# An attention and MLP kernel in which the first chunk's blocks travel before the second chunk's loads

## The chip, the cores and the metric

The kernel runs on one core of a Trainium2 chip. The metric is the time of one execution on the device in microseconds (us), the median of several runs. The data are float32 throughout.

## The reference

Two stages follow each other. The first is a recurrence (rwkv7) over 768 tokens, for 4 batches of 8 heads with 40 channels; the second is an MLP with a SiLU over all 3072 rows of 320 channels (8 heads x 40), with 2048 hidden channels.

```python
for t in range(S):
    y[:, :, t] = einsum('bhd,bhde->bhe', rt, state)
    Sa = einsum('bhde,bhe->bhd', state, at)
    state = state * wt[:, :, None, :] - einsum('bhd,bhe->bhde', Sa, bt) + einsum('bhd,bhe->bhde', vt, kt)
...
x = y.transpose(0, 2, 1, 3).reshape(B * S, H * D)
h = x @ w_in
out = (h * (1.0 / (1.0 + exp(-h)))) @ w_out
```

The two weight matrices come as 64-bit floats; the kernel gets them as pairs of 32-bit words.

## The kernel before

**Tiling.** The recurrence is cut into 12 chunks of 64 tokens. A chunk has two units (two batches each), which the code calls `units[n][m]`. Within a chunk the recurrence becomes a triangular system of 64 x 64 per batch and head; its inverse is built, and only the state goes from chunk to chunk.

**A chunk's steps and the engines they use.**
- *load* (L200, L215): a (256 KB), b and k (two halves of 128 KB each), w (two halves of 128 KB); *load_rv* (L442) brings v in two layouts (v2, vl), its transpose (vut) and r.
- *pre* (L247): `scale` makes running products of w by two scans (L254) and a reciprocal (L255) on VectorE, and multiplies a and b by them on GpSimd (L256, L257). `keys` does the same for k (L263) and sums squares on ScalarE (L266, L267). `scores` makes 64 x 64 products on TensorE (L230), masks them on VectorE into `sb` (L238), and, after the second unit, sends their 32 x 32 diagonal blocks to the DRAM tile `md` in four DMAs (L278).
- *inverse* (L295): `mi` is read back from `md` (L310), so that a block lies in one partition. For the first four chunks 15 row steps of one multiplication and one reduction each (L316, L322) on VectorE invert 16 x 16 halves; `back` turns the result, half on ScalarE (L330), half on VectorE (L331), and writes it to the DRAM tile `xd` (L332).
- *merge* (L337): four DMAs read `xd` into `XT` (L347), four VectorE transposes follow (L353), then products and copies that make 32 x 32 inverses of the 16 x 16 ones (L360 to L398, with VectorE at L368 and L393), and 64 x 64 ones of those (`first` L410 and L420, `second` L427 and L437).
- *chain* (L465): `keys` transposes (L476) and copies (L477), `right` (L238 into `sk`, L498, L508), `solve` (L520 to L546), `read` (L574, L582), `write` (L606, updates of the state Gbd L619, L623, outputs yx L628, which go to DRAM), `turn` (L558, L567).
- *moe* (L642): `first` multiplies by w_in (L669, L674), takes a sigmoid on ScalarE (L677) and multiplies on VectorE into `gts` (L678); `second` multiplies by w_out (L685).
- *weights* (L157): 40 pieces of the weights are converted from 64-bit words, each by two VectorE operations (L161, L162), three of ScalarE (L163 to L165) and three of VectorE (L170, L172, L173). Pieces pass through a few tiles named `room`; when one is done, the load of a later one is issued (L176).

**What sets the order.** The main program (L745 to L821) calls these steps in the order of the code; a scheduler arranges each engine's instructions from that, once, when the program is built. `tc.issue_after(x)` keeps what is in it behind x. `weave` mixes lists of steps. `in_order` (L185) chains TensorE's MoE products; the scans and reciprocals of chunk 0 are kept in program order (L251). Chunks 0 and 1 are inverted alone, all later ones in pairs. While chunk 0 is inverted, chunk 1's `prepare` runs, so its loads and scans stand early.

**Queues.** DMAs are issued by SyncE (SP) and ScalarE (ACT). Loads are SyncE's, except the four w of chunks 0 and 1, at the very start. The transfers md, mi, xd and XT of chunks 0 and 1 are ScalarE's, which executes them between its computations; those of later chunks are SyncE's. All loads of chunks 0 and 1, of the first five pieces of weights, of r and v and of chunk 2's b and k are issued at the start with no wait other than for a place. The two queues share eight completion semaphores, each used again only when the DMA before it on it has landed.

Of the kernel before, what the change touches and what calls it, by code (L numbers as in the profile page):

```python
# [41 lines left out]
def kernel(  # L42
# [95 lines left out]
    def load_weights(n, queue=nc.sync):  # L138

        if n == 0:  # L140
            rooms["gts"] = [sb.tile([128, 2, 4 * WS], I32, name="room2", tag="gts", bufs=2) for _ in range(2)]
        if n < NG and n % 5 < 4:
            rooms[n] = rooms["gts"][n % 5 // 2][:, n % 5 % 2]
        else:
            tag = "room" if n < NG else ("room", "mi", "tmp")[n % 3]
            rooms[n] = sb.tile([128, 4 * WS], I32, name="room", tag=tag)
        for lo, hi, src in pieces[n][1]:
            raw = rooms[n][lo:hi, 0 : 2 * WS]
            queue.dma_start(raw.rearrange("p (i x) -> p i x", x=256) if len(src.shape) == 3 else raw, src)
# [30 lines left out]
    def behind(x, ins):  # L180

        info = mybir.DependencyInfo(mybir.DependencyClass.NoSync, mybir.DependencyReason.DATA)
        tc.add_manual_dep(x.ins, ins.name, info, reason="in order")

    def in_order(x):  # L185

        if "last" in issued:
            behind(x, issued["last"])
        issued["last"] = x.ins
# [10 lines left out]
    def load(u, what="abk"):  # L200
        B2 = slice(2 * u.m, 2 * u.m + 2)
        if "a" in what:
            u.a = sb.tile([128, Q, C], F32, name="a", bufs=4)
            nc.sync.dma_start(
                u.a.rearrange("p (b q) t -> p b (q t)", b=2), aT[B2, u.n].rearrange("b p c -> p b c")
            )
        if "b" in what:
            u.kb = sb.tile([128, Q, 2, C], F32, name="kb", bufs=6)
        for n, x in ((1, bT), (0, kT)):
            for be in range(2 if "kb"[n] in what else 0):  # L210
                nc.sync.dma_start(
                    u.kb[:, P * be : P * be + P, n], x[2 * u.m + be, u.n].rearrange("p (q t) -> p q t", q=P)
                )

    def load_w(u, at, queue=nc.sync):  # L215
        u.w = at
        for be in range(2):
            queue.dma_start(
                at[:, P * be : P * be + P, 1 : C + 1], wT[2 * u.m + be, u.n].rearrange("p (q t) -> p q t", q=P)
            )  # L220

    def between(u, n, s):
# [14 lines left out]
        for j in range(2):  # L237
            nc.vector.tensor_tensor(  # L238
                out=s[:, j],
                in0=pm[j][:, 0 : P * C].rearrange("p (q t) -> p q t", q=P),  # L240
                in1=ms[:, n].unsqueeze(1).to_broadcast([128, P, C]),
                op=ALU.mult,
            )

    sbs, mark = {}, {}

    def pre(u, md):  # L247
        def scale():
            u.W = sb.tile([128, Q, C + 1], F32, name="W", bufs=6)
            R = u.w[:, :, 1 : C + 1]  # L250
            pin = tc.keep_in_program_order if u.n == 0 else lambda x: x  # L251
# [6 lines left out]
            if u.n > 0:  # L258
                keys()
# [9 lines left out]
        def scores():  # L269
# [3 lines left out]
            queue = nc.scalar if u.n < 2 else nc.sync  # L273
            for be in range(2 if u.m == NM - 1 else 0):
                for c in range(2):
                    at = 64 * (u.n % 2) + 16 * (2 * be + c)
                    r = C * be + 32 * c
                    x = queue.dma_start(  # L278
# [3 lines left out]
                    if u.n == 1:  # L282
                        behind(x, mark["mi"])
# [4 lines left out]
        return [scale, scores] + ([keys] if u.n == 0 else [])  # L288
# [6 lines left out]
    def inverse(md, N, queue, lo=0, hi=128):  # L295
# [13 lines left out]
        for h in range(lo, hi, 64):  # L309
            mark["mi"] = queue.dma_start(mi[h : h + 64], md[h : h + 64]).ins  # L310
        L = slice(lo, hi)

        def row(t):
            n = N - 1 - t
            part = tmp[L, :, 0:n, 0:n]
            nc.vector.tensor_tensor(  # L316
# [5 lines left out]
            last = nc.vector.tensor_reduce(out=X[L, :, t + 1 : N, t], in_=part, axis=AX.X, op=ALU.add)  # L322
            mark["row"] = last.ins
# [4 lines left out]
        def back():  # L328
            turned = XI.rearrange("p t s -> p s t")
            nc.scalar.copy(out=mi[L, 0:16], in_=turned[L, 0:16])  # L330
            nc.vector.tensor_copy(out=mi[L, 16:32], in_=turned[L, 16:32])  # L331
            queue.dma_start(xd[L], mi[L])  # L332
# [4 lines left out]
    def merge(n, xd, queue):  # L337
# [4 lines left out]
        def fetch():  # L342
            for be in range(2):
                at = 64 * (n % 2) + 32 * be
                for c in range(2):
                    r = C * be + 32 * c
                    queue.dma_start(  # L347
                        X[r : r + 32, :, 32 * c : 32 * c + 32],
                        xd[at + 16 * c : at + 16 * c + 16].rearrange("q s t -> s q t"),
                    )  # L350
            for r in range(0, 128, 32 if small(n) else 64):
                c = r % 64
                nc.vector.transpose(out=X[r : r + 32, :, 32 - c : 64 - c], in_=X[r : r + 32, :, c : c + 32])  # L353

        def sixteen(s, pp):

            pa = bank("pq")
# [10 lines left out]
            nc.vector.tensor_scalar(  # L368
                out=pp, in0=pa[:, 0 : N * 16].rearrange("p (h t) -> p h t", h=N), scalar1=lower, scalar2=None, op0=ALU.mult
            )  # L370
# [21 lines left out]
            for r in range(0, 128, 64):  # L392
                nc.vector.tensor_tensor(  # L393
                    out=X[r : r + 32, :, 32:48], in0=pe[r : r + 32, 1], in1=X[r : r + 32, :, 32:48], op=ALU.add
                )
# [4 lines left out]
        def first():  # L400
            s = sbs[n].rearrange("p m j q t -> p (m j q) t")
            both = sb.tile([128, N, 48], F32, name="qq", tag="tmp")
            box["qq"] = both[:, :, 0:32]
            if small(n):
                sixteen(s, both[:, :, 32:48])
# [12 lines left out]
            for be in range(2):  # L418
                R = slice(C * be + 32, C * be + 64)
                nc.scalar.copy(out=box["qq"][R], in_=pq[be][R, 0 : N * 32].rearrange("p (h t) -> p h t", h=N))  # L420

        def second():
            po = [bank("po") for _ in range(2)]
            for h in range(N):
                for be in range(2):
# [3 lines left out]
                        lhsT=box["qq"][r + 32 : r + 64, h, :],  # L429
# [9 lines left out]
        return [fetch, first, second]  # L439


    def load_rv(u):  # L442
        u.v2 = sb.tile([128, H, D], F32, name="v2", bufs=2)
        u.r = sb.tile([128, Q, C], F32, name="r", bufs=2)
# [5 lines left out]
        for be in range(2):  # L450
            nc.sync.dma_start(u.v2[C * be : C * be + C].rearrange("p h d -> p (h d)"), v[2 * u.m + be, T, :])
        for be in range(2):
            nc.sync.dma_start(
                u.vl[0:C, P * be : P * be + P, :, 0:D].rearrange("s p j d -> s (p j) d"),
                v[2 * u.m + be, T, :].rearrange("s (h d) -> s h d", d=D),
            )
        for be in range(2):
            nc.sync.dma_start(
                u.vut[:, P * be : P * be + P, 0], vT[2 * u.m + be, u.n].rearrange("p (q t) -> p q t", q=P)
            )  # L460
        nc.sync.dma_start(
            u.r.rearrange("p (b q) t -> p b (q t)", b=2), rT[B2, u.n].rearrange("b p c -> p b c")
        )

    def chain(u, xs):  # L465
# [4 lines left out]
        def keys():  # L470
            u.kt = sb.tile([128, Q, 128], F32, name="kt", bufs=2)
            for i in range(2):
# [4 lines left out]
                nc.scalar.copy(out=u.kt[:, 4 * i : 4 * i + 4].rearrange("p q e -> p (q e)"), in_=pt)  # L477

        def right():
# [26 lines left out]
            for be in range(2):  # L506
                R = slice(C * be, C * be + C)
                nc.scalar.copy(  # L508
                    out=rhs[R, :, :, 0:D],
                    in_=pr[be][R, 0 : H * D].rearrange("p (q j d) -> p q j d", q=P, j=2),  # L510
                )

# [207 lines left out]
    def invert(n, chunks=2):  # L720
# [11 lines left out]
        def do(k, i):  # L732
            if i == 0:
                box[k] = merge(k, box["xd"], queue)
            box[k][i]()

        late[n if chunks == 1 else n - 1] = [partial(do, n, 1), partial(do, n, 2)]
# [4 lines left out]
            + [partial(do, k, i) for k in each[:-1] for i in (1, 2)]  # L742
# [8 lines left out]
    for u, at in zip(units[0] + units[1], [w0] + early):  # L751
        load_w(u, at, nc.scalar)
    for n in range(2):
        for what in "ab", "k":
            for u in units[n]:
                load(u, what)
    for n in range(3):
        load_weights(n)
    for u in units[0]:
        load_rv(u)  # L760
    for n in range(3, 5):
        load_weights(n)
    for u in units[2]:
        load(u, "bk")
    convert = [partial(weights, n) for n in range(NW + 1)]

# [5 lines left out]
    run(prepare(1))  # L772
    chains = {0: [chain(u, xs) for u in units[0]]}
    run([x[i] for i in range(2) for x in chains[0]])
    run(convert[0:4] + rows[1:17])
    queue = []
    with tc.issue_after(mark["row"]):
        run(rows[17:])
        rows = invert(1, 1)
        run(late.pop(0))  # L780
        run(rows)
        for u in units[2]:
            load(u, "a")
        steps = [x for pair in zip(*[x[2:] for x in chains[0]]) for x in pair]
        steps[6:6] = late.pop(1)
        weave(steps, convert[4:21])
        for u in units[1]:
            load_rv(u)
# [6 lines left out]
        issued["last"] = mark["right"].ins  # L795
# [8 lines left out]
    for n in range(2, NN):  # L804
        for u in units[n]:
            load_rv(u)
# [170 lines left out]
```

## Time and profile before

| | |
|---|---|
| median of 5 runs | 953.76 us (952.9 to 960.2) |
| the profiled execution | 957.42 us, span 955.3 us |
| mean granted clock of TensorE | 0.918 |
| TensorE (PE) busy | 828.0 us, 87% |
| VectorE (DVE) busy | 565.8 us, 59% |
| ScalarE (ACT) busy | 291.2 us, 30% |
| GpSimd (POOL) busy | 97.4 us, 10% |
| data moved | 83.06 MB, 87 GB/s in the mean |

The profile counts an engine as busy while it computes; issuing a DMA is not counted. A page has the span in 40 slices of 23.9 us, where a digit is the busy share in tenths; windows give the same in microseconds for stretches that one chooses, with the number of instructions in brackets. The chain of waits goes back from the last instruction: each row is a start, a duration, and what the next row waited for. Groups and tiles give the durations of single instructions.

### The profile page before, as it was taken

What the parts mean: (1) busy time and instruction counts of PE and PEld (TensorE: products, weight loads), DVE (VectorE), ACT (ScalarE), POOL (GpSimd) and SP (SyncE); (2) the same over time, 40 slices, a digit from 0 to 9 for tenths busy, and PEclk for the clock granted to TensorE, in tenths of its full rate; (3) what the DMA queues carried; (4) which work ended last, traced back from release to release, by engine and by line L of the source; (5) the groups of instructions that cost most, each with busy time, mean ns of one, the idle gap of its engine ahead of it and who ended that gap; (6) DMA issues with size and microseconds to landing.
All of it is one profiled execution on the core that took longest, in us unless ns stands there. A gap on an engine that the chain in (4) does not pass through costs nothing.

```text
span 955.3 us, 26541 instructions
## 1 busy us (share of the span) xinstructions
PE 828.0 (87%) x11586; PEld 584.0 (61%) x11586; DVE 565.8 (59%) x1141; ACT 291.2 (30%) x661; POOL 97.4 (10%) x98
## 2 busy tenths in 40 slices
PE   0418379979999979999989999989999999999996
PEld 0418367746778735786637866548765477755544
DVE  8797885896216698265993457971649713031120
ACT  2436156451334212433113342124321142210110
POOL 7210022010001110001010020100110000000000
PEclk9855557899979999999999999999999989999998
DMA  9873524653126430345512655313523303002001
GB/s 219 196 166 102 121 70 112 164 122 76 42 52 145 104 95 20 94 109 127 141 25 48 146 121 117 72 44 85 134 57 82 70 17 73 2 13 62 1 0 31
DMA packets 217626, 83.06 MB, mean 87 GB/s; under 512 B 181536, under 2 KB 209440, under 8 KB 217504
## 3 DMA queue, kind: packets, MB, share of 16 engines
q1 hardware_dynamic: 204512, 78.16, 34.1%
q10 hardware_dynamic: 12992, 3.15, 1.9%
q8 instruction: 92, 1.51, 0.7%
q14 instruction: 30, 0.25, 0.1%
HBM read 67.11 MB, written 14.16 MB: 85 GB/s over the span
## 4 chain that ended last, share of the span: by engine, by line
PE 52%; DVE 33%; issue 6%; DMA 4%; POOL 2%; ACT 2%; SPq 1%; ACTq 0%; POOLq 0%; DVEq 0%
PE po L685 12%; PE ph L669 10%; DVE tmp L316 7%; DVE XI L322 7%; PE pl L574 5%; PE ph L674 3%; DVE w L255 3%; DVE gts L678 3%; PE pu L520 3%; DVE W L254 2%; PE pr L498 2%; PE pm L230 2%; PE pt L476 2%; PE pq L410 2%; PE pgy L606 2%
## 5 line engine op out<-in xcount | busy, mean ns | idle before, releaser
L685 PE MATMUL po<-wo_s,gts 128*128 128x320 f32 x768 | 223.0, 443 | 3.3 <-DVE gts L678 3.2
L669 PE MATMUL ph<-xt,wi_s 128*128 128x512 f32 (+1 forms) x448 | 194.2, 568 | 22.7 <-DVE gts L678 19.1
L685 PEld LDWEIGHTS po<-wo_s,gts 128*128 128x128 f32 x768 | 142.7, 191 | 66.3 <-DVE gts L678 6.5
L669 PEld LDWEIGHTS ph<-xt,wi_s 128*128 128x128 f32 x448 | 82.2, 198 | 107.7 <-issue 54.4
L678 DVE TENSOR_TENSOR gts<-ph,sg 128x512 f32<-128x512 f32 (+1 forms) x112 | 65.6, 607 | 136.6 <-ACT sg L677 136.4
L677 ACT ACTIVATE sg<-ph 128x512 f32<-128x512 f32 (+1 forms) x112 | 54.6, 533 | 226.2 <-PE ph L674 225.9
L316 DVE TENSOR_TENSOR tmp<-XI,mi 64x2 f32<-64x2 f32 (+40 forms) x169 | 80.9, 479 | 8.9 <-DMA mi<-md 4.5
L255 DVE RECIPROCAL w<-W 128x512 f32<-128x512 f32 x24 | 80.3, 3347 | 1.1
L322 DVE TENSOR_REDUCE XI<-tmp 64x2 f32<-64x2 f32 (+40 forms) x169 | 76.3, 452 | 4.0
L230 PE MATMUL pm<-a,kb 64*64 64x64 f32 x1536 | 48.2, 240 | 29.9 <-POOL kb L257 28.9
L230 PEld LDWEIGHTS pm<-a,kb 64*64 64x64 f32 x1536 | 38.9, 147 | 41.6 <-POOL kb L257 31.5
L238 DVE TENSOR_TENSOR sk<-pm,ms 128x256 f32<-128x256 f32 x48 | 18.4, 419 | 77.2 <-PE pm L230 77.1
L674 PE MATMUL ph<-xt,wl_s 64*128 64x512 f32 (+1 forms) x224 | 61.0, 590 | 0.0
L257 POOL TENSOR_TENSOR kb<-kb,w 128x512 f32<-128x512 f32 x24 | 29.1, 1213 | 287.3 <-DVE w L255 212.7
L256 POOL TENSOR_TENSOR a<-a,W 128x512 f32<-128x512 f32 x24 | 29.0, 1209 | 270.2 <-DMA a<-in_aT 168.3
L574 PEld LDWEIGHTS pl<-r,vut 64*128 64x128 f32 x768 | 49.4, 202 | 5.1 <-issue 2.4
L574 PE MATMUL pl<-r,vut 64*128 64x64 f32 x768 | 50.7, 288 | 1.7 <-DVE vl L582 1.6
L360 PE MATMUL pq<-XT,sb 16*32 16x16 f32 x512 | 9.1, 196 | 46.3 <-DVE XT L353 23.0
L567 ACT COPY GT<-pt 40x512 f32<-40x512 f32 x44 | 25.5, 580 | 67.0 <-PE pt L558 66.4
L582 DVE TENSOR_TENSOR vl<-pl,ml 128x512 f32<-128x512 f32 x48 | 31.1, 685 | 24.8 <-PE pl L574 24.7
L606 PE MATMUL pgy<-vl,kt 128*64 128x104 f32 (+1 forms) x768 | 41.0, 262 | 0.0
L254 DVE TENSOR_TENSOR_SCAN W<-w,one 128x260 f32<-128x260 f32 x48 | 35.1, 751 | 8.6 <-DMA w<-in_wT 8.6
(90 smaller groups left out, 1048.2 us busy)
## 6 DMA issues: line engine op xcount, KB each, us to landing
a<-in_aT SPq DMA_DIRECT2D x24, 256.0 KB
kb<-in_bT SPq DMA_DIRECT2D x48, 128.0 KB
kb<-in_kT SPq DMA_DIRECT2D x48, 128.0 KB
vut<-in_vT SPq DMA_DIRECT2D x48, 128.0 KB
r<-in_rT SPq DMA_DIRECT2D x24, 256.0 KB
w<-in_wT SPq DMA_DIRECT2D x40, 128.0 KB
room<-in_w_out SPq DMA_DIRECT2D x20, 256.0 KB
room<-in_w_in SPq DMA_DIRECT2D x16, 256.0 KB
```

The source lines that it names most:

```text
L230: nc.tensor.matmul(pm[j][C * be : C * be + C, p * C : p * C + C], lhsT=u.kb[J, q, n, :], rhs=u.a[J, q, :], start=True, stop=True,)
L254: pin(nc.vector.tensor_tensor_scan(W, w, one.rearrange("p q t -> p (q t)"), 0.0, ALU.mult, ALU.add))
L255: pin(nc.vector.reciprocal(R, u.W[:, :, 1 : C + 1]))
L316: nc.vector.tensor_tensor(out=part, in0=X[L, :, t + 1 : N, t + 1 : N], in1=M[L, :, t, t + 1 : N].unsqueeze(2).to_broadcast([hi - lo, I, n, ...
L322: last = nc.vector.tensor_reduce(out=X[L, :, t + 1 : N, t], in_=part, axis=AX.X, op=ALU.add)
L574: nc.tensor.matmul(pl[j][:, q * C : q * C + C], lhsT=u.vut[J, q].rearrange("p n t -> p (n t)"), rhs=u.r[J, q, :], start=True, stop=True,)
L606: nc.tensor.matmul(pgy[be][J, p * N + last * D : p * N + N], lhsT=u.kt[:, P * be + p, J], rhs=u.vl[:, P * be + p, j, last * D :], start=u. ...
L669: in_order(nc.tensor.matmul(ph[n], lhsT=wi_s[:, k, at : at + 128], rhs=xt[:, k, :], start=k == 0, stop=False))
L674: in_order(nc.tensor.matmul(ph[n], lhsT=wl_s[R, i, :], rhs=xt[R, 2, :], start=False, stop=True))
L677: nc.scalar.activation(out=sg, in_=ph[n], func=AF.Sigmoid)
L678: nc.vector.tensor_tensor(out=place(2 * i + n), in0=ph[n], in1=sg, op=ALU.mult)
L685: in_order(nc.tensor.matmul(po[:, 0:DM], lhsT=place(f)[:, b * 128 : b * 128 + 128], rhs=wo_s[:, NF // 2 * half + f, :], start=f == 0, stop ...
```

## The change

Chunk 0's transfers come first, and chunk 1's loads behind them:
- At the start only chunk 0's w, a, b, k, three pieces of weights and v2 are loaded; unit 0's w goes half on each queue.
- Chunk 1's fourteen loads (w, a, b, k; 2 MB) go to ScalarE's queue, in program order behind chunk 0's md and mi.
- vl, vut and r of chunk 0 and pieces 3 and 4 of the weights wait for the same point as mi (a dependency with a semaphore on the DMA of `mi`, at the first of them); what follows on SyncE stays behind. v2 stays early.
- Chunk 0's md are two on ScalarE and two on SyncE, its XT too; chunk 2's b and k are loaded after XT.
- ScalarE's DMAs are chained in one order ("scalar"); the copies kt and RHS of chunk 0 stand behind the last of the loads. SyncE's are chained from chunk 0's md on ("sync").
- VectorE's scans, reciprocals, masks, rows, transposes and merge operations of chunks 0 and 1 are chained in one order ("vector"): chunk 0's rows are one stretch, chunk 1's scans come after them, between the late steps of chunk 0's merge, which is split into five steps. Three pieces of weights instead of four are begun ahead of the rows.
- GpSimd's product with k is put later for chunk 1 as it was for chunk 0 (`keys` as a step of its own).

```diff
-    def in_order(x):
+    def in_order(x, line="moe"):
-        if "last" in issued:
-            behind(x, issued["last"])
-        issued["last"] = x.ins
+        if line in issued:
+            behind(x, issued[line])
+        issued[line] = x.ins
...
+    def send(queue, out, in_):
+        x = queue.dma_start(out, in_)
+        if queue is nc.scalar:
+            in_order(x, "scalar")
+        elif "sync" in issued:
+            in_order(x, "sync")
+        return x
...
+            if n == 1 and u.n < 2:
+                in_order(x, "vector")
...
-            pin = tc.keep_in_program_order if u.n == 0 else lambda x: x
+            pin = partial(in_order, line="vector") if u.n < 2 else lambda x: x
...
-            queue = nc.scalar if u.n < 2 else nc.sync
             for be in range(2 if u.m == NM - 1 else 0):
+                queue = nc.scalar if u.n == 1 or u.n == be == 0 else nc.sync
...
-                    if u.n == 1:
-                        behind(x, mark["mi"])
+                    if queue is nc.sync:
+                        mark["md"] = x.ins
...
-                    queue.dma_start(
+                    send(
+                        nc.sync if n == 0 and be == 1 else queue,
                         X[r : r + 32, :, 32 * c : 32 * c + 32],
...
-        return [fetch, first, second]
+        return [fetch, turned] + ([corners, complete] if small(n) else []) + [first, second]
...
+            if wait is not None and be == 0:
+                behind(x, wait, mybir.DependencyClass.Sync)
...
-                nc.scalar.copy(out=u.kt[:, 4 * i : 4 * i + 4].rearrange("p q e -> p (q e)"), in_=pt)
+                x = nc.scalar.copy(out=u.kt[:, 4 * i : 4 * i + 4].rearrange("p q e -> p (q e)"), in_=pt)
+                if u.n == 0:
+                    behind(x, issued["scalar"])
...
-    for u, at in zip(units[0] + units[1], [w0] + early):
-        load_w(u, at, nc.scalar)
+    w = [w0] + early
+    for u in units[0]:
+        load_w(u, w[u.m], (nc.scalar, nc.sync if u.m == 0 else nc.scalar))
+        load(u, "ab")
+    for u in units[0]:
+        load(u, "k")
     for n in range(2):
-        for what in "ab", "k":
-            for u in units[n]:
-                load(u, what)
-    for n in range(3):
         load_weights(n)
     for u in units[0]:
-        load_rv(u)
-    for n in range(3, 5):
-        load_weights(n)
-    for u in units[2]:
-        load(u, "bk")
+        load_v(u)
+    load_weights(2)
...
     rows = invert(0, 1)
     run(rows[0:1])
-    run(prepare(1))
+    for u in units[1]:
+        load_w(u, w[NM + u.m], (nc.scalar, nc.scalar))
+        load(u, "ab", nc.scalar)
+    for u in units[1]:
+        load(u, "k", nc.scalar)
+
+    issued["sync"] = mark["md"]
+    wait = mark["mi"]
+    for u in units[0]:
+        load_r(u, wait)
+        wait = None
+    for n in range(3, 5):
+        load_weights(n)
     chains = {0: [chain(u, xs) for u in units[0]]}
     run([x[i] for i in range(2) for x in chains[0]])
-    run(convert[0:4] + rows[1:17])
+    run(convert[0:3] + rows[1:17])
     queue = []
     with tc.issue_after(mark["row"]):
         run(rows[17:])
-        rows = invert(1, 1)
-        run(late.pop(0))
-        run(rows)
+        steps = prepare(1)
+        for u in units[2]:
+            load(u, "bk")
+        one_by_one = late.pop(0)
+        run(steps[0:1] + one_by_one[0:2] + steps[3:4] + one_by_one[2:3] + [steps[i] for i in (1, 4, 2, 5)])
+        run(one_by_one[3:])
+        run(invert(1, 1))
         for u in units[2]:
             load(u, "a")
+        del issued["sync"]
         steps = [x for pair in zip(*[x[2:] for x in chains[0]]) for x in pair]
         steps[6:6] = late.pop(1)
-        weave(steps, convert[4:21])
+        weave(steps, convert[3:21])
         for u in units[1]:
-            load_rv(u)
+            load_v(u)
+            load_r(u)
```

`load_rv` is cut into `load_v` (v2) and `load_r` (vl, vut, r); `load` takes a queue; the steps of the merge (`turned`, `corners`, `complete`) hold the operations that `fetch` and `first` held.

## The prediction

> **What bounds the kernel now.** I read the slices of the span first, then windows of it, then the chain of waits over the first 115 us, then the groups and single tiles of VectorE.
>
> ```profile
> PE   0418379979999979999989999989999999999996
> DVE  8797885896216698265993457971649713031120
> PEclk9855557899979999999999999999999989999998
> DMA  9873524653126430345512655313523303002001
> ```
>
> A slice is 23.9 us. From the tenth (about 217 us) TensorE is nearly always busy at full clock, so what happens later only hands on a lead. Before that TensorE is half idle and VectorE is busy.
>
> ```profile
> core 0: us, PE busy (x) PEld busy (x) DVE busy (x) ACT busy (x) POOL busy (x), PEclk, DMA share, GB/s
> 30.00:40.00 10.00, 7.67 (x144) 6.99 (x144) 4.78 (x15) 2.30 (x6) 1.44 (x2) 1.00 0.95 208
> 54.00:64.00 10.00, 0.00 (x0) 0.00 (x0) 9.46 (x22) 2.65 (x8) 1.17 (x1) 0.50 1.04 220
> 84.00:110.00 26.00, 19.31 (x256) 18.91 (x256) 21.98 (x61) 10.45 (x28) 0.00 (x0) 0.57 0.36 88
> 139.00:164.00 25.00, 22.49 (x365) 19.90 (x362) 15.98 (x32) 15.74 (x37) 4.84 (x4) 0.70 0.41 117
> 204.00:217.00 13.00, 7.78 (x32) 4.53 (x32) 12.40 (x27) 4.86 (x14) 2.37 (x2) 0.94 0.44 114
> ```
>
> Up to 64 us the transfers are at their limit (208 to 220 GB/s); VectorE idles 5.2 us of 30 to 40; 204 to 217 is VectorE again, TensorE idle for 5.2 us. The chain says what those transfers delay:
>
> ```profile
> 33.54 6.07 DMA mi<-md
> ...
> 60.83 3.35 DVE w L255
> 64.18 0.56 DVE XT L353
> ...
> 75.85 0.42 DVE XT L393
> 76.41 0.66 PE pq L410 x9
> ...
> 109.45 0.51 DVE mi L331
> ...
> 163.69 0.42 DVE gts L678
> ...
> 206.23 3.35 DVE w L255
> ```
>
> Chunk 0's blocks come back as mi only at 39.6; a reciprocal of chunk 2 stands before its transposes; chunk 0 is merged at about 84.7, chunk 1's rows end at 109.4, MoE's first product leaves VectorE at 163.69, and a reciprocal at 206 holds MoE up.
>
> **What the Trainium skill says.** "DMA: Bandwidth & Descriptors", Issuing engines are not separate DMA queues: transfers of SyncE and ScalarE run on the same 16 engines and interleave, and a second issuer saves issue time alone. So taking chunk 1's loads to ScalarE's queue helps only by making them later. The trace agrees: mi, on ScalarE's queue, took 6.07 us beside SyncE's loads. The same page, Anatomy of one DMA: about 2 us of a DMA are fixed, mostly the receipt of the write, and the wait for a semaphore is on the issuing sequencer. That page prices a path issued by GpSimd; here, in a quieter stretch, chunk 3's last md was issued at 204.2 and its mi, which waits for it, at 205.3, so 1.1 to 1.5 us. "SBUF — State Buffer", Who interferes with whom: VectorE and GpSimd share a port pair, and the second to issue blocks for the other's whole instruction. The trace agrees: the conversion of L161 takes 1.20 us beside a GpSimd product at 24.5 and 0.28 alone.
>
> **The change part by part.** Times against the profiled execution (957.42 us, span 955.3; it lies 3.7 above the median of the five runs, 953.76). VectorE's and ScalarE's positions are those of the built programs' orders; the new times are estimates from the durations named.
>
> 1. Blocks of chunk 0. Now: sb of unit 1 ends about 23, three md issues go at 23.6 to 24.6, the fourth waits 4.5 us for a free semaphore, mi goes at 33.54 and lands at 39.6. After: both reciprocals of chunk 0 end at about 16.3 (3.35 each, 6.95 to 10.3, 12.9 to 16.3), then two conversions (0.28+0.29+3x0.335 = 1.6 each), sb of unit 0 (2x0.4), 0.9 of a third, sb of unit 1: 22, with a conflict with GpSimd or two (1 us each) in it. Chunk 1's scans and reciprocals (4.7 a unit) no longer stand there. Four md over two queues, nothing else in the rings: landed at 24.8 by 1.5 us and a spread of issues; mi 2.5 to 3.5 more: rows start at 27.5 to 28.5 for 39.6, **-11** (-9 if the ring isn't quiet, -12.5 if sb is early).
>
> 2. Rows of chunk 0: 30 steps of 10.1 us together, spread by conversions over 13.5; now contiguous: end at 38, for 53.1.
>
> 3. ScalarE's queue. Fourteen loads (2 MB) are issued behind mi from 25.3 on; four transfers of this queue are in flight, as all eight completion semaphores are shared with SyncE. SyncE issued twelve such loads in 6.75 us (11.06 to 17.81) when it had the ring alone. Bounds: 32 us (by 7 us and free semaphores) to 46 (four at a time, each 5 to 6 us as mi was); I take 40, from 2 MB beside 1.3 MB of r and v at 210 GB/s. **Queued behind**: four kt copies (4x0.58), two RHS copies (2x0.42), the mi copy (1.08). So xd goes at 44 for 54.27, -10; VectorE waits for nothing there, since five conversions fill the gap.
>
> 4. Fetch and corners. xd to XT issue was 4.58 us in full rings, 3.0 in quiet ones (110.22 to 113.20). After: 4.3, and two queues halve the 2.23 us of four issues. The 3.35 of chunk 2's reciprocal is gone from the front of the transposes: they start at 51 for 64.1. From there to L393 11.75 us before; after, scan and reciprocal of chunk 1's unit 1 (4.7) are pinned ahead of L393, seven conversion steps (2.3) stand behind the transposes, and what stood there before (L161 at 1.23, others) is gone: 11.5. So L393 at 62.5 for 75.85, **-13**. Then ScalarE gets the four md issues of chunk 1 between the two qq copies, one of them with a wait as at 24.6 (up to 4.6): X(0) at 75 for 84.7, **-9.5** (-6 to -11).
>
> 5. Rows of chunk 1 waited for TensorE and their shared tile (83.60), with mi long there. After: mi of chunk 1 needs md of sb(11), which follows L393: sb at 66 to 68, md issue by 73, landed 75, mi at 77.5. Start -6. They took 25.5 us among chunk 0's chain; four more Gbd, two GbW and two yx (4x0.33+2x0.49+2x0.42 = 3.1) now fall inside, and the L172 of one piece waits for ScalarE: 27.5. End at 105 for 109.1, **-4**.
>
> 6. To MoE. Of the 54.6 us from there to the first gts, 37.9 are work of VectorE (38.5 after); chunk 1's sk waited for a reciprocal at 140.5 and a w at 137.97 (3.4): those are ready earlier now, so a further -2 to -4. First gts at 156.5 for 163.69, **-7** (-3 to -9).
>
> 7. Given back. VectorE's own work ahead of a point, before and after: last row of chunk 1 82.2 and 76.8; gts 1 120.1 and 115.3; gts 9 154.7 and 154.7; gts 17 176.4 and 174.6. Hence 4.8 us of conversions move behind the first gts. Between gts 1 and gts 9 VectorE had 5.5 us of idle for them (40.1 us with 34.6 of work); I count 3 us hidden, **+2**. Chunk 4's reciprocal, 3.35 on the chain at 206, goes among the rows of chunks 2 and 3: **-1** of the 5.8 us that TensorE waits around there for gts. Sum at 217 us: -7+2-1 = -6, and the rest is TensorE's.
>
> Nothing: r, vl and vut wait for mi (landed by 45; first wanted at L574, 90.9, then about 80); pieces 3 and 4 wait likewise (wanted at 39; if late, 1 us); chunk 2's loads behind XT on SyncE (wanted at 130); splitting the merge.
>
> Forecast: 957.4-6 = 951.4 for a profiled execution, **947.5** for the median.
>
> **The rivals.**
> - Given back whole: VectorE's throughput decides. For: its work up to gts 17 falls by 1.8 us only, and it is busy 174 of 210 us. Then -1.8 and what the reciprocal saves: 951 to 956, say 952.5. Against: it idles 20 us between 76 and 164.
> - Full lead: the -9.5 of X(0) goes through to rows of chunk 1, GpSimd and ScalarE free: 941 to 945. Against: step 5's round trip of md and mi begins only after chunk 0's corners.
> - Slower: ScalarE stands. Four in flight, each 6 us as mi had: the 14 loads end at 46 or later. Then copies and xd at 51, transposes at 58, L393 at 69.5, the md of chunk 1 at 80, its mi at 85, rows until 112.5: +3; the 4.8 us of deferred conversions are then on top, since chunk 1's chain has no lead to hide them: +5 to +8, 959 to 962. It decides from ScalarE free after 46 us or rows of chunk 1 starting after 84. For: L278 was seen to wait 4.5 us for a semaphore. Against: the twelve loads in 6.75 us.
>
> **How the numbers follow.** Forecast (945 to 950): 0.42; given back 0.26; full lead 0.12; slower 0.20. Half a per cent, 4.8 us, is about what a measurement of this kernel can tell from no change: faster is under 949.0, slower over 958.5. Faster: four fifths of the forecast and the full lead, 0.46; same 0.34; slower 0.20. The range leaves out a third of the full lead and three quarters of the slower case: 942 to 959.
>
> **What would show it.** Right: first row of chunk 0 at 27 to 29, ScalarE's last load issued by 42, transposes at 50 to 52, L393 at 61 to 64, rows of chunk 1 from 77, first gts at 155 to 158, no reciprocal on the chain at 200. Wrong: mi landing after 31; ScalarE issuing after 46; rows of chunk 1 ending at 109 or later; TensorE idle over 10 us between gts 1 and gts 17.

## The result, and the profile after

The changed kernel is slower by 0.8%: a median of 961.37 us (954.43 to 967.49, 42 runs) for 954.36 us (945.34 to 968.25, 79 runs of the kernel before); the ratio is 1.0083, 95% interval 1.0068 to 1.0098. The profiled execution took 963.35 us, span 961.5 us, mean granted clock 0.938. A ratio leaves out runs more than 1.5% above the fastest of the same kernel; where that matters, the medians of all runs stand beside it.

The four slices that were shown of before, now of after (one is 24.0 us):

```profile
PE   3347078979999939999989999899999999999996
DVE  8777888876216798166993548961549823031120
PEclk9999558989859979999999999998999999999999
DMA  6965615643115530455512554313422213002001
```

The start looks better: the DMA row falls from 9 to 6 in the first slice, and PEclk has two slices with a 5 there instead of four. But the fifteenth slice (336 to 360 us) has a 3 in PE's row, where before has a 7, and the twelfth (264 to 288) a 5 in PEclk's, for a 7. Windows of the kernel after; the columns are those of the windows of before:

```profile
30.00:40.00 10.00, 0.00 (x0) 0.00 (x0) 9.00 (x30) 0.00 (x0) 0.00 (x0) 1.00 1.21 232
54.00:64.00 10.00, 4.89 (x265) 4.36 (x266) 9.87 (x19) 1.33 (x4) 2.26 (x3) 1.00 0.89 236
84.00:110.00 26.00, 7.76 (x128) 6.81 (x126) 24.53 (x67) 9.76 (x26) 0.00 (x0) 0.76 0.49 123
139.00:164.00 25.00, 21.68 (x422) 18.44 (x418) 19.43 (x42) 20.91 (x52) 4.80 (x5) 0.91 0.47 131
204.00:217.00 13.00, 13.00 (x50) 8.80 (x49) 11.76 (x31) 4.94 (x15) 0.78 (x1) 0.90 0.31 64
```

From 30 to 40 VectorE does nothing but chunk 0's thirty row steps. From 204 to 217 TensorE is full, where it stood for 5.2 us of 13 before. The chain of waits of after, start and duration in us:

```profile
22.29 3.89 DMA md<-sb
26.20 3.65 DMA mi<-md
...
46.53 3.79 DMA xd<-mi
...
56.31 0.69 DVE XT L371
...
105.54 0.44 DVE room L172
106.00 0.61 DVE mi L344
...
155.18 0.76 DVE gts L707 x2
...
212.80 3.34 DVE w L263
...
227.31 1.11 ACT mi L343
228.43 4.44 DMA xd<-mi
232.89 2.07 DMA XT<-xd
234.98 0.71 DVE XT L371
```

mi takes 3.65 us for 6.07, the first gts comes at 155.18 for 163.69, and no reciprocal stands ahead of the gts near 206. It stands at 212.80 instead, inside the rows of chunks 2 and 3, and behind those rows come ScalarE's half of `back`, two transfers and the transposes of the pair: a chain in which TensorE has no part, and MoE only two additions of its outputs (L726) and two gts among the rows.

Single instructions of both traces give the lead at each point:

| | before, us | after, us | difference |
|---|---|---|---|
| first row of chunk 0 | 39.63 | 29.88 | -9.8 |
| first addition of L393 (after L416) | 75.85 | 67.10 | -8.8 |
| first and last row of chunk 1 | 83.60, 109.09 | 81.56, 105.51 | -2.0, -3.6 |
| first gts | 163.69 | 155.18 | -8.5 |
| ninth gts | 203.84 | 200.51 | -3.3 |
| seventeenth gts | 229.93 | 224.26 | -5.7 |
| rows of chunks 2, 3: first, end | 215.40, 228.49 | 209.45, 227.28 | -6.0, -1.2 |
| first transpose of chunks 2, 3 | 235.98 | 234.98 | -1.0 |
| second row of chunks 4, 5 | 330.89 | 333.50 | +2.6 |
| first transpose of chunks 4, 5 | 386.13 | 388.05 | +1.9 |
| end of the span | 955.3 | 961.5 | +6.2 |

At the seventeenth gts the lead is about the one that was forecast; the loss lies between 210 and 390 us, and again behind that. What lies there shows in TensorE's waits from 330 to 360 us (who waits, for what, total us, times, longest), of after:

```profile
PE ph L698 <- DMA xt<-xs: 9.6, 1, 9.6
PE ph L698 <- DVE gts L707: 4.9, 1, 4.9
```

and of before:

```profile
PE ph L669 <- DVE gts L678: 3.6, 2, 3.4
PE ph L669 <- DMA xt<-xs: 2.2, 1, 2.2
PE po L685 <- DVE gts L678: 1.2, 1, 1.2
```

In this stretch VectorE does the rows of chunks 4 and 5, so the recurrence gives TensorE nothing, and MoE of chunks 2 and 3 can begin only when their output has come back from DRAM (xs). What TensorE does meanwhile is whatever is left of MoE of chunks 0 and 1: 64 products with w_out (L685, L714), which stand in the trace as 128 records (each product leaves two: 768 records for the 384 products of the whole kernel). At the second row of chunks 4 and 5, 96 of these records were done before, 116 after. The reserve is 12 records instead of 32; TensorE is busy 15.53 of 30 us for 23.01. The second loss is the clock, in windows of before:

```profile
244.00:252.00 8.00, 7.67 (x267) 5.62 (x266) 3.04 (x6) 2.67 (x7) 0.66 (x2) 1.00 0.03 6
252.00:260.00 8.00, 7.99 (x209) 7.18 (x208) 1.50 (x4) 4.32 (x9) 0.00 (x0) 1.00 0.18 45
260.00:268.00 8.00, 6.85 (x290) 5.33 (x290) 0.49 (x2) 0.84 (x2) 3.40 (x4) 0.71 0.66 166
268.00:276.00 8.00, 8.00 (x157) 5.84 (x151) 0.83 (x2) 2.93 (x7) 0.00 (x0) 0.50 0.17 37
276.00:284.00 8.00, 8.00 (x262) 7.51 (x263) 1.18 (x3) 4.29 (x11) 0.00 (x0) 0.94 0.02 4
```

and of after:

```profile
244.00:252.00 8.00, 6.77 (x280) 5.18 (x280) 2.47 (x5) 3.08 (x9) 0.12 (x1) 0.93 0.01 4
252.00:260.00 8.00, 8.00 (x172) 7.45 (x171) 1.51 (x4) 3.80 (x8) 0.00 (x0) 0.64 0.03 7
260.00:268.00 8.00, 7.17 (x295) 5.92 (x290) 1.24 (x3) 1.68 (x4) 3.40 (x4) 0.78 0.73 187
268.00:276.00 8.00, 7.64 (x191) 5.94 (x184) 0.83 (x2) 2.89 (x8) 0.00 (x0) 0.50 0.24 54
276.00:284.00 8.00, 8.00 (x198) 7.29 (x201) 1.51 (x4) 2.94 (x8) 0.00 (x0) 0.50 0.01 2
```

With merge and chain of chunks 2 and 3 in it, 230 to 300 us has 13.7 us at half clock before and 27.3 after. The Trainium skill ("TensorE: Matmul & The Clock Gate", Part 1: The HAM clock gate) says that the clock is either half or full, set by activity in free-running windows of 3413 ns. The trace agrees: it has no other values, and each episode but the last, which the end cuts off, lasts a multiple of 3.4 us (20.5 us, six of them, the one from 264.6 in after).

### The profile page after: what moved, and what is told of

The parts are those of the page before. It is cut to its first block, busy times and chain, and to the rows that moved or that the text cites. A ratio compares the mean times of both kernels' runs of the same rounds, so it can differ in the third digit from the quotient of the medians.

```text
span 961.5 us, 26530 instructions
## 1 busy us (share of the span) xinstructions
PE 827.3 (86%) x11586; PEld 583.2 (61%) x11586; DVE 564.0 (59%) x1141; ACT 290.6 (30%) x661; POOL 97.4 (10%) x98
## 4 chain that ended last, share of the span: by engine, by line
PE 56%; DVE 30%; DMA 5%; issue 4%; ACT 2%; SPq 1%; POOL 1%; ACTq 0%; POOLq 0%; DVEq 0%
PE po L714 14%; PE ph L698 11%; DVE tmp L327 6%; DVE XI L334 5%; PE pl L603 4%; PE ph L703 4%; DVE w L263 3%; PE pm L236 3%; PE pt L501 3%; PE pq L429 2%; PE pr L525 2%; PE pu L549 2%; DVE gts L707 2%; PE po L446 2%; DVE Gbd L648 2%
## 5 line engine op out<-in xcount | busy, mean ns | idle before, releaser
L714 PE MATMUL po<-wo_s,gts 128*128 128x320 f32 x768 | 220.9, 440 | 4.8 <-DVE gts L707 4.8
L714 PEld LDWEIGHTS po<-wo_s,gts 128*128 128x128 f32 x768 | 141.9, 190 | 66.5 <-DVE gts L707 6.9
L327 DVE TENSOR_TENSOR tmp<-XI,mi 64x2 f32<-64x2 f32 (+40 forms) x169 | 80.9, 479 | 13.7 <-DMA mi<-md 10.1
L525 PE MATMUL pr<-v,sk 64*64 64x40 f32 x768 | 34.5, 234 | 16.1 <-ACT kt L502 14.9
L525 PEld LDWEIGHTS pr<-v,sk 64*64 64x64 f32 x768 | 29.8, 141 | 22.0 <-ACT kt L502 15.0
```

Of the source, the lines that this page charges most:

```text
L327: x = nc.vector.tensor_tensor(out=part, in0=X[L, :, t + 1 : N, t + 1 : N], in1=M[L, :, t, t + 1 : N].unsqueeze(2).to_broadcast([hi - lo, I ...
L525: mark["right"] = nc.tensor.matmul(pr[be][R, p * 80 + j * D : p * 80 + j * D + D], lhsT=u.sk[R, j, p, :], rhs=u.v2[R, 2 * p + j, :], start ...
L714: in_order(nc.tensor.matmul(po[:, 0:DM], lhsT=place(f)[:, b * 128 : b * 128 + 128], rhs=wo_s[:, NF // 2 * half + f, :], start=f == 0, stop ...
```

## The experiments

The theory at the start: the lead is lost because a scheduler, given the new start, places MoE and other work differently behind the ninth gts. Rivals: the split of the merge does it; chunk 4's reciprocal among the rows does it; ScalarE's loads do it. "Kept back" below means that 96 records of MoE's products with w_out are done at the second row of chunks 4 and 5, "ahead" that 107 to 128 are; "order" is that of the instructions on TensorE and VectorE. Ratios are to the kernel before, with the 95% interval in brackets.

**The split of the merge undone for chunks 2 to 11** (chunks 0 and 1 keep theirs):

```diff
-        return [fetch, turned] + ([corners, complete] if small(n) else []) + [first, second]
+        late = ([corners, complete] if small(n) else []) + [first]
+        if n > 1:
+            return [partial(run, [fetch, turned]), partial(run, [place] + late), second]
+        return [fetch, turned] + late + [second]
```

> The changed kernel, but for chunks 2 to 11 the merge is again three steps, as in the kernel before. Theory order (the faster start is real, and is lost because every engine's later instructions stand in another order, which the scheduler chose from the new start): VectorE's built order stays that of the changed kernel but for a few places, so 958 to 963 us and first gts at 155, gts 33 at 355 or later. Theory split (the five steps shift where the merge falls among the chain and MoE): 949 to 953. Theory start (the start is itself no gain outside the profile): 959 to 963.

Measured: 973.16 us, ratio 1.0213 (1.0174 to 1.0253); the profiled execution, span 963.8, lay under the others. VectorE's order in the trace is that of after but for some 60 of 1141 instructions, and MoE is ahead (116). The split isn't the cause; undoing it costs another per cent, which I can't place and which none of the three expectations had.

**The two halves exchanged.** One kernel has the start of after and, from the ninth gts on, the order of before on TensorE and VectorE (the merge as in the experiment above); the other has the start of before, the merges of later chunks split, and the later order of after. The order is a table, tied by dependencies that need no semaphore:

```diff
+LINES = {"vector": "123 117 124 198+3 ...", "tensor": "258+24 522+8 ..."}
...
+    for engine, line in LINES.items():
...
+        for x, y in zip(line, line[1:]):
+            tc.add_manual_dep(y, x.name, info, reason="in order")
```

> The kernel of e1, with VectorE's and TensorE's instructions from the ninth gts on pinned in the order that the kernel before has; all that comes earlier is the changed kernel's. Theory order: the lead of 5 us at gts 17 goes through to the end: 947 to 951 us, rows of chunks 2 and 3 at about 210, first gts of chunks 2 and 3 at about 345. Theory split: the same as e1, 949 to 953. Theory start: 954 to 961, no lead at the end.

> The kernel before, with the merge of chunks 2 to 11 in five steps, and VectorE's and TensorE's instructions from the ninth gts on pinned in the order that the changed kernel has. Theory order: slower than both, by the 11 us that the changed kernel loses after 217 us against the kernel before, less what the order gains by fitting another start: 960 to 967 us. Theory start: 953 to 956, as the kernel before.

Measured: after's start with before's order 959.39, 1.0072 (1.0042 to 1.0102); before's start with after's order 964.00, 1.0109 (1.0057 to 1.0162). So the later order costs a per cent without the new start. The first kernel differs from that of the experiment above by the order alone, and before's order is worth 1.4% there (1.0072 for 1.0213). But the lead that was expected of it, 947 to 951 us, did not come. As a trial of that it isn't fair: its scan of chunk 4 waits for a load of w that SyncE, which isn't tied, issues late, in the waits of VectorE from 195 to 225 us:

```profile
DVE W L268 <- DMA w<-in_wT: 5.1, 1, 5.1
```

**Chunk 4's reciprocal put behind the rows of chunks 2 and 3**, with its scans; first of unit 1 alone:

```diff
+                if (u.n, u.m) == (4, 1):
+                    behind(x, mark["back"])
...
+            mark["back"] = x.ins
```

> The changed kernel, with one addition: the scans and the reciprocal of chunk 4's second unit stand behind the last row work of chunks 2 and 3, and no longer among the rows. Theory order, with the reciprocal as its first loss: rows end at 223 for 227, transposes of chunk 2 at 231 for 235, and 953 to 958 us, since TensorE's order is again the scheduler's. If the reciprocal is no part of the loss: 959 to 963. Theory start: 959 to 963.

Measured: 954.83, 0.9996 (0.9974 to 1.0019), span 953.8: the loss is gone. Transposes at 231.22 for 234.98. But the scheduler turned MoE back to 96 records as well, so two things changed. Next, both units (`if u.n == 4`):

> e3, with both units of chunk 4: their scans and reciprocals (4.7 us each) stand behind the rows of chunks 2 and 3, so that VectorE has 4.7 us less to do ahead of gts 9. Theory: VectorE is full between gts 1 and gts 9 in the changed kernel, which is why the deferred conversions took all of 5 us of the lead there. Then gts 9 comes at 195 to 197 for 200.5, the first row at 205, and the time is 948 to 953 us. Rival: gts 9 waits for TensorE or the loads of weights, and stays at 199 to 201: 953 to 957.

Measured: 953.72 (940.02 to 959.62, 14 runs), 0.9929 (0.9891 to 0.9968); the profiled one, one of its fastest, has a span of 943.9, transposes at 227.78 and the ninth gts at 198.33, between the two expectations. The medians of all runs, 953.72 and 954.49, hardly differ, so I don't count it as faster.

**The reciprocal late in other orders**: before's order tied behind after's start, and the kernel before with this one edit.

> The kernel of r1 (the changed start, VectorE and TensorE in the order of the kernel before from the ninth gts on), in which the scans and the reciprocal of chunk 4's second unit are left out of the pinned order and stand behind the rows of chunks 2 and 3, as in e3. In r1 that scan waited 5.1 us for its w, which SyncE issues late, so r1 was no fair trial. Theory order: no such wait, first row of chunks 2 and 3 at 208 to 210, transposes of chunk 2 at 230 to 232, TensorE less idle between 330 and 360 than the 14.5 us of the changed kernel, 946 to 951 us. Theory clock (what a lead in MoE saves, TensorE gives back in half-clock episodes after it has stood): 953 to 957, with the half-clock time after 217 us at 35 us or more for 27 in the kernel before.

> The kernel before, with the scans and the reciprocal of chunk 4's second unit behind the rows of chunks 2 and 3. The start is untouched. Theory order: the 4.7 us that stood ahead of gts 11 are gone, and gts 17 and the first row of these chunks come 3 us earlier, which shows how much of the changed kernel's lead at gts 17 came from that move and not from the start: 949 to 953 us. If the move is worth nothing by itself: 953 to 956.

Measured: 956.96, 1.0033 (1.0008 to 1.0057), and 965.56 (four runs), 1.0123 (1.0068 to 1.0177). In the kernel before the edit brings the seventeenth gts to 220.76 and the transposes to 229.72, leads of 9.2 and 6.3 us, with no other part of the change; the scheduler then takes MoE ahead (107) and all is lost by 390 us. The first keeps before's order: two pairs of gts between its rows and its transposes wait for ScalarE's sigmoid, 5.3 us in all, and the transposes are at 234.84 only. Both came out slower than the theory had them (946 to 951, 949 to 953), the second slower than its rival too; the first took the time of the theory of the clock, but with 28.0 us at half clock behind 217 us for the 35 that it asked for.

**Chunk 1's loads ahead of chunk 0's blocks**, still on ScalarE's queue: the rest of the change without the empty rings.

```diff
+    for u in units[1]:
+        load_w(u, w[NM + u.m], (nc.scalar, nc.scalar))
+        load(u, "ab", nc.scalar)
...
     steps = prepare(0)
...
-    for u in units[1]:
-        load_w(u, w[NM + u.m], (nc.scalar, nc.scalar))
```

> The changed kernel, with chunk 1's fourteen loads on ScalarE's queue at the very start, ahead of chunk 0's md and mi, and so in the rings together with chunk 0's loads. VectorE's fixed order and all else stay. If it is the empty rings that make chunk 0 early: first row of chunk 0 at 33 to 40 for about 30, first gts 3 to 6 us later than 155, and 961 to 966 us. If the fixed order on VectorE does it: first row by 31 and no change, 959 to 963.

Measured: 964.86, 1.0112 (1.0082 to 1.0143). Rows of chunk 0 start at 34.20, 4.3 us later than in after, yet xd goes at 46.51 (after 46.53) and the first gts is at 153.81 (155.18). In after the rows are done at 40.5, but ScalarE issues loads until 42 and copies kt and mi before xd. The empty rings gain nothing that lasts: the first gts was expected 3 to 6 us later and came 1.4 earlier. With this start both reciprocals late:

> e4 and s1 together: chunk 1's loads ahead of chunk 0's md on ScalarE's queue, and chunk 4's scans and reciprocals behind the rows of chunks 2 and 3. s1 had the earliest MoE (gts 17 at 220.6) and the latest rows of chunks 2 and 3 (215). Theory (the recurrence of chunks 2 and 3 sets the end, not MoE's progress at 217 us): the rows start at 203 to 208 and the end lies about 568 to 574 us behind the first transposes of chunk 4, whatever that gives; 945 to 955 us if these rows are early. Rival (MoE's lead decides): as early as e4's best run whatever the rows do.

Measured: 961.05, 1.0089 (1.0056 to 1.0121). The seventeenth gts is at 209.40, 20.5 us ahead of before, and the transposes of chunks 4 and 5 are still 9.3 ahead. All 128 records are done at the second row of these chunks; TensorE's waits from 330 to 360 us:

```profile
PE ph L703 <- DMA xt<-xs: 13.7, 1, 13.7
PE ph L703 <- DVE gts L712: 5.3, 1, 5.3
```

By its median, the largest lead of all comes out behind. The profiled execution is one of its fastest (954.8), and from those transposes to its end it takes 576.2 us, more than the 568 to 574 expected.

**Denser merges**: after's order, tied, with sixteen products of 128 x 256 put into the merges of chunks 2 and 3, where the next product overwrites them.

```diff
+            return [
+                nc.tensor.matmul(bank[:, 0:256], lhsT=ident, rhs=wi_s[:, 0, 0:256], start=True, stop=True).ins
+                for _ in range(FILL if n in (2, 3) else 0)
+            ]
...
+            y = fill(pa)
```

> The changed kernel, with the same order on TensorE and VectorE, and sixteen extra dense products (128 x 128 by 128 x 256, about 0.5 us each at full clock, 8 us together) that go into the PSUM banks of the merges of chunks 2 and 3 and are overwritten: two ahead of each group of its small products, where TensorE waits for VectorE. Theory clock: TensorE loses its clock around 251 to 285 us because its queue holds only small products and waits there, so with the fillers the half-clock time after 217 us falls from 58 us to 40 or less, the stretch from the first transposes of chunk 2 to its first vl falls from 52.1 us to 50 or less although work was added, and the whole is no slower than the changed kernel: 955 to 962. Rival (the clock is a consequence that costs nothing, or is random): the fillers lengthen that stretch by 4 to 8 us and the time is 965 to 970.

Measured: 964.38, 1.0096 (1.0063 to 1.0130). In the one profiled execution of each, the clock follows density: at 252 to 260 it is 1.00 for 0.64, and half clock from 230 to 300 falls from 27.3 to 17.1 us. But the stretch from the transposes of chunks 2 and 3 to the next rows takes 101.3 us for 98.5: the fillers cost more than the clock gives, so the whole kernel says nothing more. Its time lies between the two ranges; half clock from 217 to 950 us fell from 58.0 to 41.0.

**The two suspects apart**, both with after's start and split merges: after's order with chunk 4's reciprocal behind the rows, and the order of the kernel with the late reciprocal (unit 1), but that reciprocal among the rows. The edit is a table as above.

> The changed kernel with e3's move alone: the scans and the reciprocal of chunk 4's second unit stand behind the rows of chunks 2 and 3, and from the ninth gts on TensorE's order and the rest of VectorE's are pinned as in the changed kernel, where the scheduler in e3 also chose another order for TensorE. It has the order that runs MoE ahead. If the reciprocal among the rows is the loss: transposes of chunk 2 at 231, and 954 to 957 us as e3. If MoE run ahead is the loss: transposes at 231 too, but TensorE 14 us idle between 330 and 360 as in the changed kernel, at most 182 records of L685's kind at the first transposes of chunk 4 where the kernel before and e3 have 192, and 958 to 962 us. Half of each: 957 to 959.

> The other corner: TensorE's order and VectorE's as in e3, which keeps MoE back, but the scans and the reciprocal of chunk 4's second unit stand among the rows of chunks 2 and 3 as in the changed kernel. If the reciprocal is the loss: transposes of chunk 2 at 235 to 236 and 959 to 962 us. If MoE run ahead is the loss: 955 to 957 us, with 192 records at the first transposes of chunk 4.

Measured, as ratios to before:

| | MoE ahead | MoE kept back |
|---|---|---|
| reciprocal among the rows | 1.0083 (1.0068 to 1.0098), the change | 1.0024 (1.0001 to 1.0047) |
| reciprocal behind the rows | 1.0120 (1.0064 to 1.0177) | 0.9996 (0.9974 to 1.0019) |

The order alone is worth 0.6% in the first row and 1.2% in the second, with intervals apart. The reciprocal's place shows no gain alone, and at most 0.3% where MoE is kept back (the intervals overlap). The columns are whole orders: the two tables have at least 114 of 754 VectorE instructions and 164 of 4720 TensorE instructions in another place, and MoE's place alone wasn't tried. So the kernel with the reciprocal behind the rows and MoE ahead has its transposes at 236.02, not at the 231 expected: gts stand among its rows, and one ahead of the transposes waits 3.4 us for ScalarE's sigmoid. The kernel of the other corner has the 192 records at the transposes of chunks 4 and 5 that were expected if MoE is the loss, but its median, 959.55, lies in the range for the reciprocal; the kernel before took 956.35 beside it, so the ratio is what counts. TensorE's waits from 330 to 360 us tell the orders apart at a glance. MoE ahead, reciprocal behind:

```profile
PE ph L704 <- DMA xt<-xs: 9.7, 1, 9.7
```

MoE kept back, reciprocal among the rows:

```profile
PE ph L704 <- DMA xt<-xs: 1.1, 1, 1.1
PE ph L704 <- DVE gts L713: 0.8, 1, 0.8
PE po L720 <- DVE gts L713: 0.6, 1, 0.6
```

## Why the prediction was wrong

**All fourteen kernels together.** In the six with MoE kept back (before and five experiments) the wait for xs is 1.1 to 2.5 us, and every median is under 960; in the eight with MoE ahead it is 7.5 to 13.7 us, and every median is over 961. How early a kernel is at 217 us doesn't order them. Three terms make up what follows the transposes of chunks 2 and 3, each read from one profiled execution of a kernel, which can lie some us off its median (962.98 for 959.55 with the reciprocal among the rows and MoE kept back, 954.8 for 961.05 with both reciprocals late and the loads first):

- From the transposes of chunks 2 and 3 to the second row of chunks 4 and 5 it takes 93.0 us to 107.2 us. Without the kernel with fillers, a straight line through the thirteen points gives 0.40 us for each us at half clock between 230 and 300 (correlation 0.89). Before 94.9 with 13.7 us at half clock, after 98.5 with 27.3.
- From that row to the transposes of chunks 4 and 5 it is 53.7 to 55.4 us in thirteen of fourteen, whether TensorE is busy 15.5 or 27.5 us of 30: VectorE sets it, and TensorE's standing costs nothing yet.
- From there to the end TensorE is nearly always busy (idle for 23 to 25 us in all fourteen). 192 records of products with w_out are done at the transposes with MoE kept back, 176 to 182 with it ahead, and the remaining time is 569.3 us in the mean (567.8 to 571.4) against 572.8 (569.2 to 577.9). But the ranges overlap, and the clock is in this term too: it grows by 0.40 us for each us at half clock in it (correlation 0.92; 16.1 us before, 21.1 after). In the five kernels with 15.7 to 16.4 us it is 569.2 with 192 records done, and 569.1 to 571.9 with 176 to 180. So what TensorE left is worth 0 to 2.7 us there.

For the change: -1.0 at the transposes of chunks 2 and 3, +3.6 by the rows, -0.7 in them, +4.3 behind: +6.2. That the order makes the difference is shown by the exchange of orders; how its cost divides between clock, reserve and VectorE's own order is read from these regularities and wasn't tried apart. The kernel with the reciprocal among the rows and MoE kept back had 37.2 us at half clock between 230 and 300 in its profile, more than after, and still the better median.

**By the steps of the prediction.**

1. Rows of chunk 0 at 29.88 for 27.5 to 28.5: -9.8 of -11; md and mi took 3.9 and 3.65 us. Right, a little large.
2. End 40.5 for 38, contiguous. Right.
3. ScalarE's last load was issued at 41.7 for 40, and xd at 46.5 for 44. Right, but the lead of step 1 was thereby worth nothing: the kernel with loads first has the same xd. The step counts twelve loads of SyncE from 11.06 to 17.81; the trace of before has ten there.
4. Transposes at 53.5 for 51, L393's addition at 67.1 for 62.5: -8.8 for -13. The transposes have the 2.5 us of xd. The stretch behind them took 13.6 us for 11.5: in it VectorE waited 2.1 us for TensorE's products of L406, which the step had at nothing.
5. Rows of chunk 1 81.6 to 105.5 for 77.5 to 105. Start late, end right.
6. First gts -8.5 for -7. Right.
7. Given back: the lead fell by 5.2 us from the first gts to the ninth (-8.5 to -3.3) for +2. VectorE is busy 41.6 us of 45.3 between them, 35.7 of 40.1 before, so its idle time hid 0.7 us of the added work and not 3. From the ninth gts to the seventeenth, where the reciprocal was to give 1, the lead grew by 2.4 (-3.3 to -5.7). Two mis-sized terms cancel, and -5.7 at the seventeenth gts for -6 is luck. What the step left out is that a reciprocal among the rows of chunks 2 and 3 delays those rows: 17.8 us for 13.1, and the lead of 6.0 is 1.2 at their end.

**The step that failed** is the close of step 7, "and the rest is TensorE's", with the sentence it rests on, that from 217 us TensorE is "nearly always busy at full clock, so what happens later only hands on a lead". It put at nothing what the new order and the clock would do behind that point. The lead of 6.0 us at the first row of chunks 2 and 3 is 1.2 at their end; 62.0 us lie at half clock behind 217 us for 38.6; and the kernel is 2.6 us behind at the second row of chunks 4 and 5, 6.2 at its end. TensorE is busy there, but up to 390 us it has MoE to fill with, and busy isn't the same as setting the pace: the transposes wait for VectorE's rows and the round trips, and in thirteen of fourteen kernels the rows of chunks 4 and 5 take 53.7 to 55.4 us, however busy TensorE is. MoE that comes earlier has nobody waiting for it at that point; it is a reserve for 330 to 360 us, and the new order spends it sooner. The slices showed this: the fifteenth of before has a 7 in PE's row, the twelfth a 7 in PEclk's, and the prediction passed over both.

"Nothing: ... splitting the merge" held in so far as the split isn't the loss; undone, the kernel is 1.3% slower still. The slower rival had the right side and not the mechanism: ScalarE was free before 46 us and rows of chunk 1 began before 84. The sign "TensorE idle over 10 us between gts 1 and gts 17" lies right on its limit, 10.0 us for 7.7 before; none of my signs looked past 230 us.

Open: why the scheduler takes MoE ahead under some starts and not others (a late reciprocal turns it back in after and forward in before); how much of the clock in 230 to 300 us is chance; what a fair trial of before's order would give with SyncE's order tied too. No version was shown to beat the kernel before.

## What to carry to other kernels

Follow a lead to the resource that sets the pace later, and ask what the work that now comes earlier was covering: deferred work can be a reserve for the stalls to come. Where a scheduler lays out the program, an edit at the start changes the order far behind it, so compare the built orders to the end and count the reserve at each later stall. A digit below 9 in the bound engine's row, or in the row of its clock, is a place where a lead can be lost.

## What the runs showed of the hardware

- TensorE's clock dropped to half though its records fill most of the stretch: 6.77 of 8 us busy at 244 to 252, then 0.64. The page named above (HAM oscillation — how this bites in real kernels) speaks of idle gaps of over about 3.4 us; here the longest pause from 236 to 284 us is 0.83 us, and with dense fillers 252 to 260 ran at 1.00. That is one profiled execution of each kernel.
- Fourteen loads on ScalarE took from 26.75 to 42.35 us to issue, 1.1 us each, where SyncE had issued ten in 6.75. The Trainium skill ("DMA: Bandwidth & Descriptors", Issuing engines are not separate DMA queues) calls the time to issue usually small beside the DMA itself. An issue took 0.55 to 0.69 us here; the other 7 us are waits for the completion semaphores shared with SyncE. From the sixth load on, each waits for the semaphore that it uses again, and seven of these nine go within 0.03 us of the last landing on it (landing at 39.60, issue at 39.62). With the issues, this kept ScalarE from its copies for 15.6 us.
- Runs of one program spread with the clock: the 27 runs of the kernel before beside the last two experiments go from 948.8 us at a mean clock of 0.929 to 976.1 at 0.910 (correlation -0.90). Across kernels, and with the new start, the mean clock doesn't tell the time: the kernel with both reciprocals late took 941.8 us at 0.962 and 959.6 at 0.939, but its fastest run, 940.0, was at 0.929; and after is slower than before at a higher mean clock (0.938 for 0.918 in the profiled executions; up to 217 us it has 58.0 us at half clock for 117.5, behind that 62.0 for 38.6).
